# Block-sparse attention feeding a channel mixer: attention units of two query blocks of two batches, sampled values loaded by SyncE, a mixer that alternates batches

## The chip, the core and the metric

The kernel runs on one core of one Trainium2 chip. TensorE (PE) does the matrix products and the transposes, VectorE (DVE), ScalarE (ACT) and GpSimd (POOL) do the elementwise work, SyncE (SP) issues most transfers; sixteen DMA engines move the data between device memory and the on-chip memory. The metric is the time of one execution on the device in microseconds (us). A kernel's time is the median of its runs. A profiled execution also gives a span, from the first to the last instruction; the time of a run includes a little around it.

## The reference

There are 4 batches, 8 heads, 768 tokens and 64 channels a head; the tokens form 24 blocks of 32. A query block sees its own block and both neighbours, the first and the last block, and three sampled blocks; queries of the first and the last block see all keys.

```python
mask = np.abs(blk_i - blk_j) <= 1
mask = mask | (blk_i == 0) | (blk_j == 0) | (blk_i == 23) | (blk_j == 23)
for qb in range(24):
    for kb in sampled_blocks[qb]:            # three per query block, the same for all batches and heads
        mask[qb*32:(qb+1)*32, kb*32:(kb+1)*32] = True
scores = np.where(mask, 0.125 * q @ k.T, -1e9)
attn = softmax(scores)                       # row maximum taken off, sum + 1e-9 below
x = (attn @ v)                               # heads side by side: (4, 768, 512)
x_prev = x shifted by one token, zero before the first
xk = mu_k * x + (1 - mu_k) * x_prev
xr = mu_r * x + (1 - mu_r) * x_prev
kk = np.maximum(xk @ w_k, 0.0)               # 512 -> 1024
out = sigmoid(xr @ w_r) * ((kk * kk) @ w_v)  # 1024 -> 512
```

The weights come as 64-bit floats, the rest as 32-bit.

## The kernel before

**Attention units.** The work on attention is cut into units of 128 query rows. A *wide* unit (u = 0, one per batch) takes the four blocks 21, 22, 23 and 0. Blocks 21 and 22 go with the two that see all keys, and a mask does the rest; for each pair of heads (`wide_pair`) it computes scores against all 768 keys. A *near* unit (u = 1 to 5) takes four consecutive query blocks of one batch; each block of 32 rows has its own eight key blocks: three neighbours, the first and the last block, three sampled ones. `near_group` does half of the heads at a time: 32 small score matmuls per group (line 525), mask and row minimum on VectorE (line 480), exponential on ScalarE (line 490), eight transposes (line 501), their copy out (line 507), 64 value matmuls (line 547). `finish` divides by the sums (line 610), transposes (line 607) and copies into the mixer's input `xt` (line 624).

**Keys and values of a near unit.** `load_unit` brings them. For each query block SyncE issues one transfer of the three neighbour blocks' keys (line 460), one of the first and last block's keys where the slot held another batch (line 454), and three of sampled blocks (line 456), whose address SyncE works out from a register. They go into one of `KR_BUFS` = 5 slots, used in turn; a unit uses four. The neighbours' values and block 0's are one transfer by SyncE (line 469) into the first half of one of `VR_BUFS` = 6 slots; the last block's and the three sampled blocks' values are gathered by GpSimd's queue with a list of row numbers in `lines` (line 471, an indirect transfer over 128 partitions). The list is made once at the start by `find` in `mask_setup`.

**Mixer.** `mixer(b)` runs over three tiles of 256 tokens of one batch, batch after batch. A tile has two gates (`gate`, line 714), four pairs of hidden blocks (`hidden`, line 732, with ReLU at 745, square at 746, and the low part of the square at 747 and 749) and two value products (`values`, line 761), each in three terms of split precision. `split_x` makes the mixed inputs: differences (line 677, on VectorE for the tiles in `DIF_DVE`, else on GpSimd), mixes (line 681), and a high and a low part (lines 688, 690). The next tile's inputs are made during the present one. The 64-bit weights are brought by ScalarE's queue (line 352) and turned into 32-bit high and low parts by `weight` (lines 361 to 388).

**Order.** Every operation is put in a `Plan` with an engine, an expected duration, a rank and its dependences; `Plan.order` places them one after another: on each engine, among operations that can start within `NEAR` ns of the first possible one, that of lowest rank; an operation whose mode (`table`) is that of the one before is preferred by `STAY`. The order in which they are placed is the order of the instructions; on the chip each engine then works in order and waits for what it needs. `UNITS` is the order of the attention units, `unit_time` their ranks. Transfers are modelled with one rate, one delay and a completion. While TensorE has nothing to do before `SPIN_END`, idle matmuls (line 335) are put in its gaps.

`UNITS` begins with the wide units of batches 0, 1 and 2, then units 1 and 2 of batch 0, then the wide unit of batch 3, then the rest in order of batch. The results of the wide units of batches 2 and 3 are kept in device memory (`away`) until `xt` has room.

## Time and profile before

| | |
|---|---|
| median of 3 runs | 627.03 us (623.53 to 627.45) |
| profiled execution | 621.7 us span; its own time is not given apart, and the median of the runs lies 5.3 us above this span |
| PE busy | 592.3 us, 95% of the span |
| VectorE, ScalarE, GpSimd busy | 301.6, 301.5, 343.7 us |
| moved by DMA | 114.18 MB, 184 GB/s over the span |
| key transfers of sampled blocks (line 456) | 240 of 64 KB |
| value gathers by GpSimd (line 471) | 80, 79.1 us busy |

In a busy-time row by stage the columns are the stretch and its length in us, then PE, weight loads, VectorE, ScalarE, GpSimd (with the number of instructions), the granted clock, the mean share of the DMA engines and GB/s. In a timeline row they are start, duration, engine, line, operation, output and inputs, count, and in brackets the idle time before it and what ended it. In a group's row the busy time and the mean duration of one in ns stand after the first bar, the engine's idle time before these instructions after the second. A busy PE is not a PE at its peak: the ends of matmuls are modelled, and time in its pipeline counts.

### The profile page before, as it was taken

The numbers are of one execution on the slowest core, as the hardware profiler recorded it, in microseconds if no ns is written. First come the engines' busy times: TensorE is split into PE (matmuls) and PEld (weight loads), VectorE is DVE, ScalarE is ACT, GpSimd is POOL, SyncE is SP. The second block draws the span as 40 slices with busy tenths as digits, with TensorE's granted clock in tenths as the row PEclk, the third lists the DMA queues.
The fourth block names the chain that finished last, engine by engine and source line by source line (L and its number), as shares of the span: only waits on it lengthen the run. The fifth ranks groups of instructions, "written<-read, shape, count | busy, mean of one in ns | idle before, by whom it ended". The sixth has DMA issues, their size and how long they took to land.

```text
span 621.7 us, 20808 instructions
## 1 busy us (share of the span) xinstructions
PE 592.3 (95%) x8243; PEld 471.8 (76%) x8253; DVE 301.6 (49%) x906; ACT 301.5 (48%) x712; POOL 343.7 (55%) x400
## 2 busy tenths in 40 slices
PE   8799989899999999999999998999999999999997
PEld 3566655568767877877878777778778778889897
DVE  5659755787574355264353443562633531415300
ACT  3566762576643545455445535544535444243341
POOL 1215541658886647557837835546457554565551
PEclk9989999999999999999999999999999999999999
DMA  8979658948788387665765765775755620000000
GB/s 303 351 227 338 200 157 297 289 151 273 261 236 283 86 277 223 193 198 183 237 205 155 220 190 177 247 212 163 233 185 162 212 79 2 34 1 35 18 18 34
DMA packets 88499, 114.18 MB, mean 184 GB/s; under 512 B 12626, under 2 KB 59219, under 8 KB 88403
## 3 DMA queue, kind: packets, MB, share of 16 engines
q1 hardware_dynamic: 78690, 81.30, 41.1%
q0 software_dynamic: 6400, 20.98, 10.6%
q10 hardware_dynamic: 3312, 10.59, 4.9%
q8 instruction: 65, 1.06, 0.7%
q14 instruction: 32, 0.25, 0.1%
HBM read 106.01 MB, written 6.82 MB: 181 GB/s over the span
## 4 chain that ended last, share of the span: by engine, by line
PE 62%; ACT 9%; issue 7%; POOL 6%; DMA 6%; DVE 5%; SPq 2%; another core or an unknown queue 2%; ACTq 0%; POOLq 0%
PE v L761 14%; PE h_3p L732 6%; PE h_1p L732 5%; PE h_2p L732 5%; PE o L547 5%; PE r_0p L714 5%; ACT p L490 4%; PE t L501 4%; PE s L525 4%; PE r_1p L714 3%; PE h_0p L732 3%; DMA k_ring<-kq 2%; PE tw L501 2%; PE o L586 2%; POOL VR L471 2%
## 5 line engine op out<-in xcount | busy, mean ns | idle before, releaser
L761 PE MATMUL v<-wv,k 128*128 128x512 f32 (+1 forms) x600 | 140.9, 387 | 0.9 <-POOL wv L388 0.8
L761 PEld LDWEIGHTS v<-wv,k 128*128 128x128 f32 x600 | 107.1, 188 | 26.0 <-DVE xr_2f L681 1.2
L490 ACT ACTIVATE p<-p,nm 128x256 f32<-128x256 f32 x160 | 79.4, 498 | 41.8 <-DVE nm L480 35.4
L471 POOL DMA_INDIRECT VR<-vt,lines x80 | 79.1, 988 | 34.9 <-issue 15.1
L507 DVE COPY pt<-t 128x512 f32<-128x512 f32 x80 | 53.1, 685 | 68.7 <-PE t L501 65.2
L480 DVE CUSTOM_DVE_ANT_1 p<-s,near_mask 128x256 f32<-128x256 f32 x160 | 57.7, 419 | 39.2 <-remote 19.6
L690 POOL TENSOR_TENSOR xr<-xr_1f,xr 128x256 fp32r<-128x256 f32 x24 | 17.8, 740 | 69.1 <-ACT xr L688 68.9
L525 PE MATMUL s<-KR,q 64*32 64x256 f32 x1280 | 49.5, 381 | 1.3 <-issue 0.7
L501 PE MATMUL t<-ident,p 128*128 128x128 f32 x320 | 47.6, 278 | 1.0 <-ACT p L490 0.4
L547 PEld LDWEIGHTS o<-VR,pt 128*32 128x32 f32 x2560 | 37.8, 110 | 13.3 <-issue 9.5
L688 ACT CAST xr<-xr_1f 128x256 fp32r<-128x256 f32 x24 | 9.7, 406 | 73.6 <-PE r_0p L714 49.0
L547 PE MATMUL o<-VR,pt 128*32 128x64 f32 x2560 | 44.6, 221 | 0.4 <-DMA VR<-vt,lines 0.4
L732 PE MATMUL h_1p<-xk,wk 128*128 128x256 f32 x288 | 37.0, 283 | 8.0 <-ACT h_0k L745 4.7
L610 DVE TENSOR_TENSOR x<-o,R 128x512 f32<-128x512 f32 x24 | 16.6, 691 | 56.9 <-PE o L547 51.3
L501 PEld LDWEIGHTS t<-ident,p 128*128 128x128 f32 x320 | 36.0, 141 | 8.8 <-ACT p L490 5.5
L732 PEld LDWEIGHTS h_1p<-xk,wk 128*128 128x128 f32 x288 | 34.7, 188 | 10.4 <-ACT h_0k L745 5.6
L490 ACT ACTIVATE pw<-pw,nmw 128x768 f32<-128x768 f32 x32 | 29.8, 935 | 21.0 <-DVE nmw L480 16.2
L732 PEld LDWEIGHTS h_0p<-xk,wk 128*128 128x128 f32 x288 | 34.9, 188 | 3.4 <-issue 2.9
L732 PEld LDWEIGHTS h_2p<-xk,wk 128*128 128x128 f32 x288 | 34.9, 188 | 3.4 <-ACT k L746 2.9
L732 PE MATMUL h_3p<-xk,wk 128*128 128x256 f32 x288 | 37.1, 283 | 0.2 <-ACT h_2k L745 0.2
L525 PEld LDWEIGHTS s<-KR,q 64*32 64x32 f32 x1280 | 25.9, 105 | 14.8 <-issue 6.2
L732 PE MATMUL h_2p<-xk,wk 128*128 128x256 f32 x288 | 37.0, 283 | 0.0
(115 smaller groups left out, 1078.6 us busy)
## 6 DMA issues: line engine op xcount, KB each, us to landing
VR<-vw SPq DMA_DIRECT2D x80, 256.0 KB
KR<-kd SPq DMA_DIRECT2D x80, 192.0 KB
KR<-kt SPq DMA_DIRECT2D x240, 64.0 KB
k_ring<-kq SPq DMA_DIRECT2D x16, 384.0 KB
VR<-vt SPq DMA_DIRECT2D x24, 256.0 KB
q<-qt SPq DMA_DIRECT2D x23, 256.0 KB
out<-z SPq DMA_DIRECT2D x23, 256.0 KB
early_w<-w_k ACTq DMA_DIRECT2D x8, 512.0 KB
```

Source lines behind the costliest of these rows:

```text
L471: plan.add(POOL, GATHER, at - LEAD_V + 0.01 * j, lambda w=w, n=n: nc.gpsimd.indirect_dma_start(VR[w].ap[:, 1, :], None, vt.rearrange("b n ...
L480: nc.vector.tensor_tensor_reduce(out=p.ap[:, cs].rearrange("p (a x) -> p a x", x=BLK), in0=view().rearrange("p (a x) -> p a x", x=BLK), in ...
L490: plan.add(ACT, 280 + 0.83 * (cs.stop - cs.start), rank, lambda: nc.scalar.activation(p.ap[:, cs], p.ap[:, cs], AF.Exp, bias=nm.ap[:, col ...
L501: nc.tensor.transpose(tp.ap[:, i, :], p.ap[:, cs], ident.ap)
L507: plan.add(DVE, 600, rank + 0.1, lambda: nc.vector.tensor_copy(out=pt.ap, in_=tp.ap), reads=[(tp,)], writes=[(pt,)])
L525: nc.tensor.matmul(s.ap[ROWS[j], row, a * 256 : (a + 1) * 256].rearrange("p (n x) -> p n x", x=BLK), q.ap[half, hp, ROWS[j]], KR[keys[j]]. ...
L547: nc.tensor.matmul(o.ap[ROWS[j], h * D : (h + 1) * D], pts[i // 2].ap[:, 2 * (i % 2) + g, ROWS[j]], VR[values[j]].ap[:, g, h * D : (h + 1) ...
L610: plan.add(DVE, 600, rank, lambda: nc.vector.tensor_tensor(out=x.ap.rearrange("p (h d) -> p h d", d=D), in0=o.ap.rearrange("p (h d) -> p h ...
L690: plan.add(POOL, 80 + 2.4 * MIX * tw, rank + O_MIX, lambda f=f, cs=cs: nc.gpsimd.tensor_tensor(out=dst.ap[:, 1, cs], in0=f.ap, in1=dst.ap[ ...
L714: nc.tensor.matmul(pr.ap[:, 0:512], xr.ap[:, a, c, :], wr.ap[:, w, c, :], start=(c == 0 and m == 0), stop=(c == CC - 1 and m == 2))
L732: nc.tensor.matmul(ph.ap[:, ff * TT : (ff + 1) * TT], wk.ap[:, w, c, f * P : (f + 1) * P], xk.ap[:, a, c, :], start=(c == 0 and m == 0), s ...
L761: nc.tensor.matmul(pv.ap[:, 0:width], k2.ap[:, a, f, i * P : (i + 1) * P], wv.ap[:, w, f, cs], start=(f == 0 and m == 0), stop=(f == FC - ...
```

## The change

A near unit becomes two query blocks of two batches (a pair), so there are 10 units for each of the 2 pairs, still of 128 rows and with the same matmuls. A key slot holds eight blocks of both batches: twice as large, `KR_BUFS` = 2 instead of 5. A sampled key block of both batches is one transfer of 128 KB where there were two of 64 KB. A value slot holds one set of four blocks for both batches, and a unit uses two for the neighbours (one transfer of 512 KB each) and two for the last and the sampled blocks. Those are now issued by SyncE, three transfers of 128 KB a slot, each to 32 of the 128 partitions, with the same register as the keys; the last block's is brought again only where the slot held something else. GpSimd issues no gather, and `lines`, `find` and their input are gone.

The input of the mixer is kept by pair and tile of 256 tokens (three buffers of both batches) instead of by batch. The copy into it is cut in two where a unit lies across two tiles. The mixer goes through the tiles in the order (0, t0), (1, t0), (0, t1), (1, t1), (0, t2), (1, t2), (2, t0), (3, t0) and so on. The wide units stay what they were; the order of units begins with the wide ones of batches 2, 0 and 1, then the first four near units of the first pair, then the wide one of batch 3. The planner models eight transfers in flight at a time, prices leaving a mode of TensorE by the mode that is left, and all its ranks are new. All differences of the mixer's inputs are on GpSimd (`DIF_DVE` is empty). The masks of all near units are made by whole-tile instructions.

```diff
-QB, NC, SLOTS = 4, 5, 8
+QB, SLOTS = 4, 8
+PAIR = 2
+NP, NM = B // PAIR, (NB - QB) // PAIR
...
-    SWITCH = {"ACT": 1300, "PE": 110}
+    SWITCH = {"ACT": 1300}
+    LEAVE = {"scores": 300, "values": 170, "wide": 110, "whole": 90}
...
-    RING, RING_POOL, RATE, DONE = 650, 1000, 310, 670
+    RING, RATE, DONE, LANES = 650, 300, 670, 8
...
+            if op.size:
+                end = at
+                for i in range(op.parts):
+                    end = max(end, lanes[lane]) + ns / op.parts
+                    queue_free = max(queue_free, end + self.RING) + op.size / op.parts / self.RATE
+                    lanes[lane] = queue_free + self.DONE
+                    lane = (lane + 1) % self.LANES
...
-UNITS = [(0, 0), (1, 0), (2, 0), (0, 1), (0, 2), (3, 0)]
-UNITS += [(b, u) for b in range(B) for u in range(1, NC + 1) if (b, u) not in UNITS]
+UNITS = [
+    (2, ALL), (0, ALL), (1, ALL), (0, 0), (0, 1), (0, 2), (0, 3), (3, ALL), (0, 4), (0, 5), (0, 6), (0, 7),
+    (0, 8), (0, 9), (1, 0), (1, 1), (1, 2), (1, 3), (1, 4), (1, 5), (1, 6), (1, 7), (1, 8), (1, 9),
+]
+TILES = [(PAIR * p + i, t) for p in range(NP) for t in range(NT) for i in range(PAIR)]
...
-    KR = [fixed([P, SLOTS, HP * BLK], F32, f"KR{i}") for i in range(KR_BUFS)]
-    VR = [fixed([P, 2, DM], F32, f"VR{i}") for i in range(VR_BUFS)]
+    KR = [fixed([P, SLOTS, PAIR, HP * BLK], F32, f"KR{i}") for i in range(KR_BUFS)]
+    VR = [fixed([P, PAIR, DM], F32, f"VR{i}") for i in range(VR_BUFS)]
...
                 for i in range(NRAND):
-                    nc.sync.dma_start(KR[r].ap[:, 5 + i, :], kt[bass.ds(sampled_block(n, i) + b * NB, 1)].rearrange("o p x -> p (o x)"))
+                    nc.sync.dma_start(KR[r].ap[:, 5 + i].rearrange("p b x -> p (b x)"),
+                                      kt[bass.ds(sampled_block(n, i) + pr * NB, 1)].rearrange("o p x -> p (o x)"))
...
-            plan.add(SP, ISSUE, at - LEAD_V + 0.01 * j, lambda w=w, n=n: nc.sync.dma_start(VR[w].ap[:, 0, :], vw[b, n - 1]),
-                     writes=[(VR[w], 0)], release=at - LEAD_V, size=262144)
-            plan.add(POOL, GATHER, at - LEAD_V + 0.01 * j, lambda w=w, n=n: nc.gpsimd.indirect_dma_start(
-                VR[w].ap[:, 1, :], None, vt.rearrange("b n k x -> (b n k) x"),
-                bass.IndirectOffsetOnAxis(ap=lines.ap[:, b, n - 1 : n], axis=0)),
-                reads=[(lines,)], writes=[(VR[w], 1)], release=at - LEAD_V, size=262144)
+            def gather(w=far, n=n, more=more):
+                if more:
+                    nc.sync.dma_start(VR[w].ap[0:BLK].rearrange("p b x -> p (b x)"), vt[(pr + 1) * NB - 1].rearrange("k b x -> k (b x)"))
+                for i in range(NRAND):
+                    nc.sync.dma_start(VR[w].ap[(i + 1) * BLK : (i + 2) * BLK].rearrange("p b x -> p (b x)"),
+                                      vt[bass.ds(sampled_block(n, i) + pr * NB, 1)].rearrange("o k b x -> (o k) (b x)"))
+            plan.add(SP, ISSUE, at - LEAD_V + 0.01 * j, lambda w=near, n=n: nc.sync.dma_start(VR[w].ap.rearrange("p b x -> p (b x)"), vw[pr, n - 1]),
+                     writes=[(VR[near], 0, 1)], release=at - LEAD_V, size=524288)
...
-                            q.ap[half, hp, ROWS[j]], KR[keys[j]].ap[half, :, hp * BLK : (hp + 1) * BLK],
+                            q.ap[half, hp, ROWS[j]], KR[keys[j % PAIR]].ap[half, :, j // PAIR, hp * BLK : (hp + 1) * BLK],
...
-                            VR[values[j]].ap[:, g, h * D : (h + 1) * D], start=(g == 0), stop=(g == 1), skip_group_check=True)
+                            VR[values[j % PAIR][g]].ap[:, j // PAIR, h * D : (h + 1) * D], start=(g == 0), stop=(g == 1), skip_group_check=True)
...
-KR_BUFS, VR_BUFS, P_BUFS, PT_BUFS, T_BUFS, M_BUFS = 5, 6, 4, 4, 2, 1
+KR_BUFS, VR_BUFS, P_BUFS, PT_BUFS, T_BUFS, M_BUFS = 2, 6, 4, 4, 2, 1
...
-DIF_DVE = frozenset([(2, 0), (2, 1), (3, 1), (3, 2)])
-O_MAX, O_EXP, O_TR, O_PV, O_END = -5.335, 4.852, 0.824, 2.509, 0.703
-FIRST_K, LEAD_W, LEAD_Q, LEAD_K, LEAD_V = 35.035, 14.471, 9.567, 12.128, 8.904
-O_MIX, O_SQ = -5.339, -10.806
-NEAR = 94.131
+DIF_DVE = frozenset()
+O_MAX, O_EXP, O_TR, O_PV, O_END = -18.352, 15.421, 7.927, 14.932, 5.117
+FIRST_K, LEAD_W, LEAD_Q, LEAD_K, LEAD_V = 32.834, 15.273, 22.533, 12.051, 10.413
+O_MIX, O_SQ = 24.788, -13.071
+NEAR = 308.526
...
-A_FIRST, A_WIDE, A_SOON, A_STEP = 4.254, 17.894, 6.977, 20.726
-SOON, SECOND = 3, 0.36
-STAY, STORE = 3.933, 955.319
-M_FIRST, M_STEP, M_LAST = 84.0, 41.944, 446.907
+A_FIRST, A_WIDE, A_SOON, A_STEP = -6.908, 16.07, 11.323, 23.999
+SOON, SECOND = 8, 0.264
+STAY, STORE = 7.732, 0.0
+M_FIRST, M_STEP, M_LAST = 83.39, 40.819, 510.717
```

More of the change, by code (lines that the diff above doesn't have):

```diff
@@ L148, in order @@
                 for op in ops:
-                    at = max(now, op.release)
-                    for d in op.deps:
-                        at = max(at, d.end + (self.HOP[d.engine] if d.engine != engine else self.SAME.get(engine, 60)) + d.lag)
+                    at = max(now, op.ready)
                     for buf in op.bufs:
@@ L217, in block_sparse_attention_channel_mix @@
     ctx: ExitStack, tc: tile.TileContext,
[L218 removed]
+    kt, kd, kq, qw, qn, vt, vw, blocks, rows, consts, mu_k, mu_r, w_k, w_v, w_r, out, wide,
 ):
@@ L447, in load_unit, with load_near @@
+        return q, keys, values
+    def load_near(pr, m, at):
+        q = buf([P, HP, P], F32, "q", 2, f"q{pr}_{m}")
+        plan.add(SP, ISSUE, at - LEAD_Q, lambda: nc.sync.dma_start(q.ap, qn[pr, m]),
+                 writes=[(q, *range(HP))], release=at - LEAD_Q, size=262144)
+        keys, values = [], []
+        ahead = FIRST_K if (pr, m) == (0, 0) else LEAD_K
+        for j in range(PAIR):
+            n = PAIR * m + 1 + j
             r = place(0)
             keys.append(r)
-            more = slots[r] != b
@@ new lines, in finish @@
+        pr, i = divmod(b, PAIR)
+        spans = [(0, 1, 3 * BLK, P), (NT - 1, 1 + TT - 3 * BLK, 0, 3 * BLK)]
+        if not pr:
+            for t, at, lo, hi in spans:
+                plan.add(ACT, 200 + 0.83 * CC * (hi - lo), rank, lambda t=t, at=at, lo=lo, hi=hi: nc.scalar.copy(
+                    xt[pr, t].ap[:, i, :, at : at + hi - lo], tp.ap[:, :, lo:hi]), reads=[(tp,)], writes=[(xt[pr, t], (ALL, b))])
+            return
+        to = buf([P, CC, P], F32, "pt", PT_BUFS, f"hold{b}")
@@ new lines, in finish, with back @@
+        keep = away[b - PAIR]
+        plan.add(ACT, 590, rank, lambda: nc.scalar.copy(to.ap, tp.ap), reads=[(tp,)], writes=[(to,)])
+        plan.add(SP, ISSUE, rank, lambda: nc.sync.dma_start(keep.ap, to.ap), reads=[(to,)], writes=[(keep,)], size=262144)
+        for t, at, lo, hi in spans:
+            def back(rank, t=t, at=at, lo=lo, hi=hi):
+                plan.add(SP, ISSUE, rank, lambda: nc.sync.dma_start(xt[pr, t].ap[:, i, :, at : at + hi - lo], keep.ap[:, :, lo:hi]),
+                         reads=[(keep,)], writes=[(xt[pr, t], (ALL, b))], size=262144)
+            held.setdefault((pr, t), []).append(back)
@@ new lines, in block_sparse_attention_channel_mix, with touch @@
+    held = {}
+    seen = set()
+    def touch(pr, t, rank):
+        if (pr, t) in seen:
+            return
+        seen.add((pr, t))
+        if t == 0:
+            plan.add(POOL, 50, rank, lambda: nc.gpsimd.memset(xt[pr, t].ap[:, :, :, 0:1], 0.0), writes=[(xt[pr, t], "z")])
+        for back in held.get((pr, t), ()):
+            back(rank)
+    def attention():
+        for i, (b, m) in enumerate(UNITS):
+            t0, t2 = unit_time(i), unit_time(i + 1)
+            name = f"{b}_{m}"
+            o = buf([P, DM], F32, "o", 1, f"o{name}", ps)
+            L = buf([P, H], F32, "L", 4, f"L{name}")
+            if m == ALL:
+                q, keys, values = load_wide(b, t0 if i else A_FIRST - 24)
@@ L811, in mixer @@
             plan.add(ACT, 1040, at(13), sigmoid, reads=[(z[0],), (z[1],)], writes=[(z[0],), (z[1],)], table="sigmoid")
-            for i in range(2):
-                values(b, t0, i, k2, z[i], last, at(15.6 + 5.2 * i), rate)
+            for half in range(2):
+                values(b, t0, half, k2, z[half], last, at(15.6 + 5.2 * half), rate)
     mask_setup()
@@ L817, in block_sparse_attention_channel_mix @@
     weights()
-    for b in range(B):
-        mixer(b)
+    mixer()
     before = None
```

317 lines of the change are left out of this document (144 added, 173 removed).

## The prediction

> **What bounds the kernel now.** I read the page first, for its span and its forty slices, then the busy time by stage, then the chain of waits for what one piece costs when nothing is in its way, and last the timelines of TensorE and SyncE around the place where the mixer starts.
>
> ```profile
> span 621.7 us, 20808 instructions
> ...
> PE 592.3 (95%) x8243; PEld 471.8 (76%) x8253; DVE 301.6 (49%) x906; ACT 301.5 (48%) x712; POOL 343.7 (55%) x400
> ...
> PE   8799989899999999999999998999999999999997
> ...
> DMA  8979658948788387665765765775755620000000
> ```
>
> The span is 621.7 us. The median of the runs shown is 627.03, so 5.3 us lie around the span; I make the sum on the span and add 5.3. TensorE looks busy in nearly every slice, but its record also covers waiting inside the pipeline, so I ask what it delivered. In the DMA slices the transfers are dense for the first third and absent in the last sixth.
>
> ```profile
> 0.00:121.40 121.40, 107.58 (x1966) 68.78 (x1977) 78.79 (x242) 68.66 (x152) 42.41 (x59) 0.97 0.80 270
> 121.40:139.70 18.30, 16.94 (x495) 12.24 (x493) 15.15 (x42) 12.26 (x25) 11.80 (x15) 1.00 0.52 170
> 139.70:180.00 40.30, 38.35 (x575) 30.98 (x568) 27.54 (x68) 22.28 (x57) 33.23 (x37) 1.00 0.82 258
> 180.00:520.00 340.00, 330.99 (x4567) 272.38 (x4566) 153.67 (x490) 165.50 (x422) 204.96 (x240) 1.00 0.62 193
> 520.00:621.70 101.70, 98.40 (x653) 87.41 (x651) 26.41 (x68) 32.77 (x59) 51.29 (x52) 1.00 0.06 22
> ```
>
> The columns are TensorE matmuls, weight loads, VectorE, ScalarE, GpSimd, then the clock, the DMA share and the rate. What each piece costs back to back comes from the chain of waits (start, duration, line, count), first its front and then its tail:
>
> ```profile
> 51.54 1.49 PE sw L564 x8
> ...
> 57.56 1.04 PE tw L501 x8
> ...
> 70.88 1.48 PE o L586 x96
> ...
> 96.56 1.03 PE o L547 x64
> ...
> 136.71 1.02 PE s L525 x32
> ...
> 142.83 0.44 PE tx L607 x4
> ...
> 147.62 0.87 PE t L501 x8
> ```
>
> ```profile
> 551.58 10.90 PE v L761 x48
> 562.48 2.82 PE h_0p L732 x24
> 565.30 2.80 PE r_0p L714 x12
> ```
>
> A mixer tile is 48 value matmuls (10.90), four pairs of hidden blocks (4 x 2.82) and two gates (2 x 2.80): 27.8 us. A near unit is 64 score matmuls (2 x 1.02), 16 transposes (2 x 0.87), 128 value matmuls (2 x 1.03) and its last four transposes (0.44): 6.3 us. A wide unit is 4 x 1.49 + 6 x 1.04 + 4 x 1.48 + 0.44 = 18.6 us. Twelve tiles, 20 near units and four wide ones: 333 + 126 + 74 = 533 us. So about 88 us of the span are not TensorE work, and no part of the diff changes the 533. The question is only where the 88 lie.
>
> ```profile
> 79.34 1.10 PE L525 MATMUL s<-KR,q 64*32 64x256 f32 x32 [0.48 <-PE tw L501]
> ...
> 82.35 1.66 PE L525 MATMUL s<-KR,q 64*32 64x256 f32 x32
> ...
> 86.42 1.55 PE L586 MATMUL o<-VR,ptw 128*32 128x64 f32 x96
> ...
> 101.16 1.49 PE L525 MATMUL s<-KR,q 64*32 64x256 f32 x37
> ...
> 113.65 0.60 PE L607 MATMUL tx<-ident,x 128*128 128x128 f32 x4 [0.16 <-DVE x L610]
> ...
> 121.45 3.05 PE L714 MATMUL r_0p<-wr,xr 128*128 128x512 f32 x12
> ...
> 139.73 3.10 PE L732 MATMUL h_0p<-xk,wk 128*128 128x256 f32 x24
> ```
>
> From 139.73 on, mixer work is always at hand. Before that the wide units and two near units had been done:
>
> ```profile
> 0.00:139.70 139.70, 27.94 (x1536) 23.90 (x1536) 0.98 0.76 257
> ```
>
> ```profile
> 0.00:139.70 139.70, 7.83 (x192) 3.69 (x192) 0.98 0.76 257
> ```
>
> The first row is line 586 (all 1,536 wide value matmuls are done), the second line 525 (three near units' scores). With the matching transposes and one gate (2.8) TensorE had delivered 74 + 2 x 6.3 + 2.0 + 2.8 = 91 us by 139.7: 48 us are lost in front. The tail from 520 on is TensorE work end to end (the three rows of the tail above are from there, and 551.58 + 10.90 is where the next one starts), so it loses nothing, and the other 40 us lie between 139.7 and 520.
>
> **The front, part by part.** The first mixer tile needs two near units now; in the change two batches come ready together, so it needs four, and the fourth wide unit comes after them. What paces near units in a row? Scores of one unit begin at 79.34, of the next at 101.16: 21.8 us. SyncE in between:
>
> ```profile
> 83.45 0.33 SPq L460 DMA_DIRECT2D KR<-kd  x1
> ...
> 92.64 1.69 SPq L456 DMA_DIRECT2D KR<-kt  x3
> ...
> 96.39 0.34 SPq L426 DMA_DIRECT2D q<-qt  x1
> ```
>
> After the last scores (82.35 + 1.66 = 84.0) SyncE sends the next keys from 83.45 to 94.33, then the queries at 96.39, and the scores start 4.8 us behind those. The change halves the key transfers of a unit (two neighbour and six sampled ones for 4 and 12, each twice as wide): half of those 10.9 us goes, 5.4, and the larger lead of the queries takes up to 2.0 more (96.39 - 94.33). The period becomes 14.4; if the new value transfers get in between it stays at up to 21.8. There is no spare key slot any more (two instead of five), but in the old ring, too, three of four blocks waited for the scores. Fourth near unit's scores: 79.3 + 3 x 14.4 = 122.5; last transposes 12.5 later (113.65 - 101.16), first gate 7.8 after that (121.45 - 113.65): 143. By then TensorE has done three wide units (55.7), four near units (25.1) and as much of the fourth wide unit as VectorE lets through.
>
> ```profile
> L480 DVE CUSTOM_DVE_ANT_1 p<-s,near_mask 128x256 f32<-128x256 f32 x160 | 57.7, 419 | 39.2 <-remote 19.6 <-PE s L525 16.7 <-PE r_1p L714 2.9
> L507 DVE COPY pt<-t 128x512 f32<-128x512 f32 x80 | 53.1, 685 | 68.7 <-PE t L501 65.2 <-PE o L547 2.2 <-DMA away<-hold 0.7
> ...
> L480 DVE CUSTOM_DVE_ANT_1 pw<-sw,wide_mask,nmw 128x384 f32<-128x384 f32 x32 | 18.5, 612 | 4.4 <-PE sw L564 4.2
> ...
> L480 DVE CUSTOM_DVE_ANT_1 pw<-sw,wide_mask 128x384 f32<-128x384 f32 x32 | 16.8, 552 | 4.8 <-PE tw L501 4.0 <-PE sw L564 0.6
> ```
>
> VectorE was busy 78.8 + 15.2 = 94 us up to 139.7. Two more near units add at least 2 x (57.7 + 53.1) / 20 = 11, the fourth wide unit without its masks takes away (18.5 + 16.8) / 4 = 8.8. With the whole of that wide unit VectorE would be 105 of 143 us busy, 73% against 67% now. I take two thirds of the wide unit as done, 12 us: 143 - 55.7 - 25.1 - 12 = 50 lost, against 48. I count the front at 0; its ends are -5 (the whole wide unit fits) and +14 (the rival below).
>
> **The middle.**
>
> ```profile
> L471 POOL DMA_INDIRECT VR<-vt,lines x80 | 79.1, 988 | 34.9 <-issue 15.1 <-PE o L547 14.7 <-PE o L586 2.4
> ...
> L732 PE MATMUL h_1p<-xk,wk 128*128 128x256 f32 x288 | 37.0, 283 | 8.0 <-ACT h_0k L745 4.7 <-issue 2.4 <-ACT p L490 0.9
> ...
> L677 POOL TENSOR_TENSOR xk_2d<-xt 128x256 f32<-128x256 f32 x12 | 7.2, 615 | 0.4 <-DVE xk_2f L681 0.4
> ```
>
> Sampled values no longer go through GpSimd: 80 gathers of 988 ns leave its queue, 79 us in all. What was behind them there is the preparation of the next tile (lines 677 and 690) and the squares (747, 749). Their waits:
>
> ```profile
> POOL VR L471 <- PE o L547: 14.7, 8, 8.6
> ```
>
> 14.7 us in eight waits, at most 8.6, in which GpSimd stood still with mixer work queued behind. GpSimd is 60% busy between 180 and 520 (204.96 of 340), so most of its loss is covered by TensorE's other work; if that cover is gone it is worth the whole 14.7. I take 4. Against it, the differences of four tiles go from VectorE to GpSimd: 48 operations of at most 0.62, under 30 us, beside 79 freed; nothing.
>
> The new ranks put ReLU and square ahead of the exponentials (the offset of the first falls from -10.8 to -13.1, of the second rises from 4.9 to 15.4). The second hidden block's row shows 8.0 us of idle TensorE, mostly waiting for ScalarE's first hidden block, which stands behind four exponentials. I take 6 of the 8; below, nothing; above, 8. What is late next is the transposes of that near unit, with value matmuls there to fill.
>
> The planner now prices leaving each TensorE mode and prefers longer to stay. The remaining 32 us of the middle are such changes and short waits; a tenth of it, 3, is my estimate, from a loss of 6 (exponentials too late, tiles short of work) to a gain of 8.
>
> On SyncE a unit sends 6 dynamic value transfers for 6 dynamic key transfers saved (3 take 1.69), so its time stays as it was. The added wait is that of these value transfers on the preceding value matmuls; behind it stand the next keys, the queries and the output stores, and the score matmuls wait for those. The neighbour values waited on the same matmuls at the same place before, so nothing; the other end is the 8.6 above. The extra pieces of the copy to the mixer's input (four more copies of part of a tile) lie on a ScalarE that is half idle (165.50 of 340). Alternating batches in the mixer changes no instruction; the tail still holds at least the two tiles that need the last unit, and stays full.
>
> Values now land in 32 partitions at a time.
>
> ```profile
> q0 software_dynamic: 6400, 20.98, 10.6%
> ```
>
> 20.98 MB took 10.6% of 621.7 us, 65.9 us on all engines, 3.1 us per MB. The new sampled values are 15.7 MB (120 times 128 KiB): 49 us. If a 32-partition transfer holds the engines twice as long, 49 more are spread over the span; in the middle the share is 0.62 and hides its part, in front (0.80) four units' 3.1 MB add up to 10. The Trainium skill has such a rule ("SBUF — State Buffer", Door 1: The DMA port swizzle): 32 partitions reach 8 of 16 ports, with about half the rate. No transfer of this trace is so narrow; by that rule the sum would be 624 instead of 614.
>
> **Sum.** 621.7 + 0 - 4 - 6 - 3 = 608.7, with 5.3 around it 614.
>
> **The rivals.** *More than that:* the planner's DMA lanes also keep the early key loads out of the way of the wide units, the near period falls to 11, and the gate starts at 133: with the same two thirds 40 lost, -8 in front, and 5 more of the middle: 601. For it: VectorE has room. Chance 0.17.
> *Nothing:* one set of short waits for another, 627. For it: TensorE is the bound and its 533 stay. Chance 0.20.
> *Slower: the mixer starves at its start.* The near period stays at 21.8, because SyncE now carries the values between keys. Scores of the fourth unit at 144.7, first gate at 165; TensorE has done 55.7 + 25.1 + 18.6 and some 3 of a fifth unit, 102: 63 lost, +15, and of the middle's 13 only 4 come: 638. It decides from a period of about 18.7, where 3 x 4.3 eat the 13. Against it: the key transfers are halved. Chance 0.18.
> *The narrow values* hold the engines in front, as above: 624. Chance 0.06. The forecast has 0.39.
>
> **How the numbers follow.** A measurement here can tell about 1% from no change: 620.8 and 633.3 are the bounds. The forecast's own range, 603 to 625, is faster in 0.33 of its 0.39; with the first rival and a little of the others faster gets 0.52, the same 0.27 (most of *nothing*, the narrow values, the rest of the forecast), slower 0.21. The range takes in the first rival's 601 with some room and most of the slow one: 598 to 638.
>
> **What would show it.** Near scores in the front at a period near 14 us and the first gate near 143; a GpSimd queue without gathers and with under 300 us of work; no idle time at the second hidden block; a tail of full slices after the last near unit. The prediction is wrong if the first hidden blocks come after 160, if SyncE's waits for value matmuls hold key loads, or if TensorE's lost time between there and the last unit isn't under 30 us.

## The result, and the profile after

The kernel before took 627.42 us beside it (median of 12 runs, 623.53 to 629.97), the changed kernel 623.87 (12 runs, 614.38 to 630.08). The ratio of 0.986 [0.982, 0.990], about 1.4% faster, leaves out the seven of the changed kernel's twelve runs that lie over 1.5% above its fastest; the two medians, over all runs, give 0.994. Run again later as `after2`, beside 13 runs of the kernel before (626.01), it took 622.06 (617.18 to 628.44), ratio 0.992 [0.988, 0.996], and the medians again give 0.994. So the change gains 0.6 to 1.4%, and whether it is more than 1% is not settled.

> The changed kernel once more, for a second profile beside the experiments. Both theories: a ratio near 0.986 to the kernel before; the first hidden blocks between 145 and 163 us, where the kernel before has them at 139.7; a near period of some 15 to 20 us in the front (70.6, 85.7, 105.8, 126.1 in the profile at hand).

The profile taken with the result has a granted clock of 0.983 (own time 623.73, span 622.0); the lines below are from `after2`, with 0.994 (own time 618.72, span 616.9). Its page, as for the kernel before:

```profile
span 616.9 us, 20533 instructions
...
PE 585.6 (95%) x8267; PEld 476.2 (77%) x8281; DVE 291.0 (47%) x850; ACT 300.7 (49%) x716; POOL 287.0 (47%) x360
...
PE   9999899698889999799999999999999999999997
...
DMA  8896788898879576875557447575384420000000
```

The span is 4.8 us shorter than before's 621.7, VectorE and GpSimd have less to do (291.0 and 287.0 us for 301.6 and 343.7), and the last sixth of the DMA slices is empty as before. By stage, with the cuts at the first gate, the first hidden block, 200 and 520 us (columns: TensorE matmuls, weight loads, VectorE, ScalarE, GpSimd, clock, DMA share, GB/s):

```profile
0.00:122.20 122.20, 107.53 (x2154) 71.94 (x2169) 73.84 (x235) 65.47 (x154) 26.93 (x37) 0.98 0.83 266
122.20:157.20 35.00, 31.15 (x707) 22.43 (x705) 21.96 (x71) 22.21 (x55) 9.45 (x13) 0.96 0.89 272
157.20:200.00 42.80, 37.32 (x497) 30.00 (x490) 37.48 (x90) 26.98 (x73) 29.26 (x32) 1.00 0.88 263
200.00:520.00 320.00, 316.09 (x4354) 268.12 (x4353) 138.64 (x414) 156.44 (x383) 164.42 (x208) 1.00 0.56 166
520.00:616.90 96.90, 93.48 (x569) 83.69 (x567) 19.05 (x41) 29.62 (x55) 56.90 (x71) 1.00 0.06 22
```

The timeline of TensorE shows where the mixer starts (start, duration, line, operation, count, idle time before it):

```profile
70.11 1.96 PE L538 MATMUL s<-KR,q 64*32 64x256 f32 x64
...
85.67 1.96 PE L538 MATMUL s<-KR,q 64*32 64x256 f32 x64
...
105.74 1.51 PE L538 MATMUL s<-KR,q 64*32 64x256 f32 x45
109.84 1.05 PE L538 MATMUL s<-KR,q 64*32 64x256 f32 x19 [2.59 <-issue]
...
122.29 2.83 PE L744 MATMUL r_0p<-wr,xr 128*128 128x512 f32 x6
125.04 1.96 PE L538 MATMUL s<-KR,q 64*32 64x256 f32 x64
126.93 1.67 PE L744 MATMUL r_0p<-wr,xr 128*128 128x512 f32 x6
...
157.28 3.14 PE L762 MATMUL h_0p<-xk,wk 128*128 128x256 f32 x24
```

The first gate comes at 122.29, in two halves, and the first hidden block at 157.28, against 121.45 and 139.73 before. What had been done by then, from the same busy-time view for three lines alone, the wide value matmuls (line 599), the near scores (538) and the near value matmuls (560):

```profile
0.00:157.20 157.20, 25.16 (x1488) 22.01 (x1488) 0.98 0.84 267
```

```profile
0.00:157.20 157.20, 11.02 (x320) 6.13 (x320) 0.98 0.84 267
```

```profile
0.00:157.20 157.20, 8.47 (x512) 7.50 (x512) 0.98 0.84 267
```

That is 1,488 of 1,536 wide value matmuls, the scores of five near units, the values of four and one gate: 74.4 - 0.7 + 4 x 6.3 + 2.0 + 2.8 = 103.7 us by the prices of the prediction. So 157.2 - 103.7 = 53.5 us are lost in front, where the kernel before lost 48. The 533 us of TensorE work being the same, 616.9 - 533 = 83.9 are lost in all, and 30.4 of them after the first hidden block, where it lost 40. By this pair of profiles the change costs 5 us in front and saves 10 behind. The profile taken with the result has the same work done and its first hidden block at 162.59, 5.3 us later than `after2`, and 459.4 us from there to its end, against 459.6: what the front costs differs between executions by as much as its own size.

### The profile page after: what moved, and what is told of

The parts are those of the page before. It is cut to its first block, busy times and chain, and to the rows that moved or that the text cites. A ratio compares the mean times of both kernels' runs of the same rounds, so it can differ in the third digit from the quotient of the medians.

```text
span 622.0 us, 20533 instructions
## 1 busy us (share of the span) xinstructions
PE 589.5 (95%) x8267; PEld 479.7 (77%) x8281; DVE 291.8 (47%) x850; ACT 301.0 (48%) x716; POOL 287.1 (46%) x360
## 3 DMA queue, kind: packets, MB, share of 16 engines
q1 hardware_dynamic: 51730, 96.63, 51.7%
q8 instruction: 65, 1.06, 0.7%
## 4 chain that ended last, share of the span: by engine, by line
PE 83%; DVE 6%; issue 5%; DMA 3%; SPq 2%; ACT 1%; ACTq 0%; DVEq 0%
PE v L791 20%; PE s L538 6%; PE r_0p L744 6%; PE o L560 5%; PE h_2p L762 5%; PE h_3p L762 5%; PE h_1p L762 5%; PE h_0p L762 5%; PE r_1p L744 5%; PE t L515 4%; PE tw L515 4%; PE sw L577 3%; PE idle L334 3%; DMA KR<-kt 2%; PE tx L618 2%
## 5 line engine op out<-in xcount | busy, mean ns | idle before, releaser
L791 PE MATMUL v<-wv,k 128*128 128x512 f32 (+1 forms) x600 | 137.9, 385 | 0.7 <-POOL wv L387 0.4
L538 PE MATMUL s<-KR,q 64*32 64x256 f32 x1280 | 46.8, 399 | 8.9 <-issue 6.5
L560 PE MATMUL o<-VR,pt 128*32 128x64 f32 x2560 | 42.3, 220 | 3.5 <-issue 3.3
L515 PE MATMUL t<-ident,p 128*128 128x128 f32 x320 | 44.4, 280 | 0.3 <-PE tx L618 0.2
L515 PEld LDWEIGHTS t<-ident,p 128*128 128x128 f32 x320 | 38.3, 145 | 5.3 <-ACT p L504 1.1
L799 DVE SCALAR_TENSOR_TENSOR z<-v,z 128x512 f32<-128x512 f32 (+1 forms) x25 | 16.7, 668 | 50.8 <-PE v L791 29.5
L762 PEld LDWEIGHTS h_3p<-xk,wk 128*128 128x128 f32 x288 | 36.3, 194 | 3.3 <-ACT h_2k L775 2.3
L744 PE MATMUL r_0p<-wr,xr 128*128 128x512 f32 x144 | 37.9, 412 | 0.0
L519 ACT COPY ptw<-tw 128x512 f32<-128x512 f32 x48 | 26.6, 588 | 23.1 <-PE tw L515 17.7
L762 PE MATMUL h_0p<-xk,wk 128*128 128x256 f32 x288 | 37.4, 285 | 0.2 <-ACT z L751 0.2
```

The costliest lines, as they stand in the source:

```text
L515: nc.tensor.transpose(tp.ap[:, i, :], p.ap[:, cs], ident.ap)
L519: plan.add(ACT, 490, rank + 0.1, lambda: nc.scalar.copy(pt.ap, tp.ap), reads=[(tp,)], writes=[(pt,)])
L538: nc.tensor.matmul(s.ap[ROWS[j], row, a * 256 : (a + 1) * 256].rearrange("p (n x) -> p n x", x=BLK), q.ap[half, hp, ROWS[j]], KR[keys[j % ...
L560: nc.tensor.matmul(o.ap[ROWS[j], h * D : (h + 1) * D], pts[i // 2].ap[:, 2 * (i % 2) + g, ROWS[j]], VR[values[j % PAIR][g]].ap[:, j // PAI ...
L744: nc.tensor.matmul(pr.ap[:, 0:512], xr.ap[:, a, c, :], wr.ap[:, w, c, :], start=(c == 0 and m == 0), stop=(c == CC - 1 and m == 2))
L762: nc.tensor.matmul(ph.ap[:, ff * TT : (ff + 1) * TT], wk.ap[:, w, c, f * P : (f + 1) * P], xk.ap[:, a, c, :], start=(c == 0 and m == 0), s ...
```

## Experiments

They were timed in four sets, each on one chip together with the kernel before; ratios compare within a set. In the first three the kernel before took 626.01, 624.32 and 626.74 us, in the last 610.71. Unless something else is said the order of every engine is that of the changed kernel.

**Sampled values of full width (`wide_values`).** Is a transfer to 32 partitions slow? Here each goes to all 128, 1 KB in each, so that the sampled keys meet other values.

```diff
-nc.sync.dma_start(VR[w].ap[(i + 1) * BLK : (i + 2) * BLK].rearrange("p b x -> p (b x)"),
-                  vt[...].rearrange("o k b x -> (o k) (b x)"))
+nc.sync.dma_start(VR[w].ap[:, i % 2, i // 2 * (DM // 2) : (i // 2 + 1) * (DM // 2)],
+                  vt[...].rearrange("o k b (c x) -> (o k b c) x", c=2))
```

> The sampled values are brought in the same number of transfers of the same 128 KB by the same queue in the same order, but spread over 128 partitions (rows of 1 KB) instead of 32 (rows of 4 KB), so that they stand in the wrong places and the attention's result is left wrong; nothing else changes. Theory N (the narrow transfers hold the DMA engines and the keys behind them land late): the median time to landing of these transfers falls from 5.3 us to about 4, the stall of 3.4 us inside the third near unit's scores goes, the first hidden blocks come 5 to 10 us earlier, and the time falls by 4 to 8 us, to a ratio of 0.973 to 0.980. Theory K (two key slots without a spare one pace the near units, whatever the width): the first hidden blocks stay within 3 us, the ratio within 0.004 of the changed kernel's.

615.28 us (613.43 to 618.83), ratio 0.982 [0.974, 0.990]; `after2` ran in the same set with 622.06. The median is 6.8 us lower, as the first theory had it, though the two intervals overlap; the spans of the profiles are 5.2 apart. From the two pages, `after2` first: the large queue (packets, MB, share of 16 engines) and the landing of the value transfers (count, KB each, us):

```profile
q1 hardware_dynamic: 51730, 96.63, 51.9%
...
VR<-vt SPq DMA_DIRECT2D x129, 128.0 KB, 4.9
```

```profile
q1 hardware_dynamic: 64114, 96.63, 49.5%
...
VR<-vt SPq DMA_DIRECT2D x129, 128.0 KB, 4.2
```

The same 96.63 MB held the engines 51.9% of 616.9, 320 us, and 49.5% of 611.7, 303 us; a transfer lands 0.7 us sooner. So the narrow transfers cost 17 us of engine time more than these wide ones. But the rows changed too, from 4 KB to 1 KB. The next kernel, `pool_same`, brings the sampled values in rows of 4 KB over 128 partitions, by another queue; its page:

```profile
q1 hardware_dynamic: 45538, 79.72, 38.5%
q0 software_dynamic: 5760, 20.97, 10.0%
```

Of its 619.0 us, 38.5% are 238 us for the 79.72 MB of everything else. If these cost the same in `after2`, its other 16.91 MB, the narrow values, held the engines the remaining 82 us, 4.8 us per MB, where the gathers take 62 us for 20.97 MB, 3.0 per MB; the wide rows of 1 KB come to 3.8 by the same working. By this estimate a narrow transfer holds the engines 1.6 times as long as a wide gather, some 32 us more in all, where the prediction had 49 for twice as long (the same working with `ring7_pool_ns` below gives 4.9 and 2.9 us per MB). The Trainium skill ("SBUF — State Buffer", Door 1: The DMA port swizzle) gives a transfer to partitions 0 to 31 half of the ports; the trace agrees on the direction, at 1.6 and not 2. But the first hidden block came at 155.85, only 1.4 earlier, where the theory had 5 to 10; of the 5.2 us between the spans 3.8 lie behind that block.

**Gathers by GpSimd again (`pool_same`).** All sampled values come by 40 gathers of 512 KB on GpSimd, as wide as before the change.

```diff
+lines = ...                          # row numbers, made once
-for i in range(NRAND): nc.sync.dma_start(VR[w].ap[(i + 1) * BLK : ...], vt[...])
+nc.gpsimd.indirect_dma_start(VR[w].ap..., None, vt..., IndirectOffsetOnAxis(ap=lines.ap[:, pr, n - 1 : n], axis=0))
```

> The changed kernel with its order of instructions on every other engine, but each block's sampled values of both batches come in one indirect gather on GpSimd's queue (40 of 512 KB, over 128 partitions) instead of three transfers by SyncE (120 narrow ones). My step that the gathers off GpSimd are worth 4 us: 40 gathers are half of the old 80, so 1 to 3 us are lost in the middle. Theory N: the front gains 4 to 8 us, as with full-width values, so 2 to 6 us faster than the changed kernel, ratio 0.976 to 0.983. Theory K with my step: 1 to 3 us slower, ratio 0.988 to 0.991.

619.58 us (617.49 to 621.02), ratio 0.986 [0.979, 0.993]. The group of gathers, and TensorE's first hidden block:

```profile
L494 POOL DMA_INDIRECT VR<-vt,lines x40 | 40.0, 1000 | 41.1 <-PE o L579 28.8
```

```profile
158.81 3.14 PE L781 MATMUL h_0p<-xk,wk 128*128 128x256 f32 x24
```

From 158.81 to the end of its 619.0 us are 460.2 us, with the gathers; 616.9 - 157.28 = 459.6 without. GpSimd waits 28.8 us on value matmuls in these gathers, with mixer work behind them, and TensorE loses nothing measurable by it. The ratio lies between those of the two theories, and the first hidden block is not earlier than in `after2`: neither was borne out.

**The fourth wide unit earlier (`w3_early`)**, between the second and the third near unit, planned anew:

```diff
-(0, 0), (0, 1), (0, 2), (0, 3), (3, ALL), (0, 4)
+(0, 0), (0, 1), (3, ALL), (0, 2), (0, 3), (0, 4)
```

> The fourth wide unit stands between the second and the third near unit instead of behind the fourth, with the order planned for it. If TensorE's loss in front is waiting for the keys and values of near units (both theories), the wide unit's 18.6 us of work fill it: 4 to 8 us less lost before the mixer, ratio 0.973 to 0.980. Rival (VectorE paces the front, as my two thirds of the wide unit had it): the mixer starts later by as much as is filled, and the ratio stays within 0.004 of the changed kernel's or goes above it.

637.41 us (632.05 to 639.74), ratio 1.013 [1.004, 1.022], the first hidden block at 177.68 us. The work done up to there is that of `after2` but for the 48 last wide value matmuls, so some 20 us more are lost; the granted clock is 0.93 up to there, against 0.98. Moving the wide unit forward did not fill the front. That is the sign that the rival had named, but the order was planned anew, so it does not show that VectorE paces the front.

**Fewer bytes (`light_both`, `light_free`), and no dummies (`no_spin`).** In the second to fifth near unit one sampled key block and one sampled value block are loaded instead of three; and the dummy matmuls that the planner puts into gaps of TensorE are left out after the planned 80 us.

```diff
-for i in range(NRAND):                                    # keys, and the same for values
+for i in range(1 if pr == 0 and 1 <= m <= 4 else NRAND):  # light_both, light_free
...
-if before is not None and warm.start < op.start <= cold.start:
+if before is not None and warm.start < op.start <= min(cold.start, 80e3):   # light_free, no_spin
```

> The changed kernel with two of the three sampled key loads and two of the three sampled value loads left out in the second to fifth near unit of the first pair (32 transfers of 128 KB, 4.2 MB; what an earlier unit left stands in their place, so the sampled part of those units is not computed). The order on every engine is the same, and the dummy matmuls stay. Theory (the bytes pace the front: 0.72 to 0.99 of the DMA engines' time is taken from 40 to 160 us, at 228 to 295 GB/s): 4.2 MB at 240 GB/s are 17 us, of which the dummy matmuls, whose number is fixed, keep some 7; first hidden block at 143 to 150 instead of 157.3, time 609 to 616 us. Rival (TensorE's own order, or another engine, paces the front): first hidden block at 154 to 158, time within 3 us of the changed kernel's 622 to 624.

> The same loads left out, and the 49 dummy matmuls that the changed kernel issues after the planned 80 us left out too (10.4 us of TensorE at 213 ns). Theory (bytes pace the front): first hidden block 2 to 6 us earlier than with the dummies, at 138 to 147, if the clock holds; time 606 to 614. Rival: first hidden block at 154 to 158.

> The changed kernel without those 49 dummy matmuls, all loads in. If loads are what TensorE waits for there, the dummies only fill the wait: first hidden block within 2 us of 157.3, or later by what half clock costs, time 621 to 628. Rival (the dummies, planned at one and a half times the gap, themselves delay the front): first hidden block 4 to 9 us earlier, time 612 to 618.

`light_both` took 614.48 us (ratio 0.982 [0.977, 0.988]), `light_free` 606.54 (0.969 [0.962, 0.976]), `no_spin` 618.85 (0.991 [0.987, 0.994]). Their first hidden blocks, in that order:

```profile
158.35 3.14 PE L762 MATMUL h_0p<-xk,wk 128*128 128x256 f32 x24
```

```profile
149.64 3.14 PE L762 MATMUL h_0p<-xk,wk 128*128 128x256 f32 x24
```

```profile
159.91 3.14 PE L762 MATMUL h_0p<-xk,wk 128*128 128x256 f32 x24
```

Taking 4.2 MB away does nothing for the start of the mixer (158.35), nor does taking the dummies away (159.91); both together bring it to 149.64, 10.3 earlier than without the dummies alone. That lies between the forecasts of the theory (138 to 147) and of the rival (154 to 158), though the time is as the theory had it. The dummies are a fixed number, made for the gaps of the plan. Between 70 us and the first hidden block the profiles of `after2` and `light_both` list no wait of TensorE for a DMA transfer, that of `no_spin` 4.5 us, that of `light_free` 0.5. So with the dummies in its queue TensorE does not wait for loads, and without them it does. Of the 10.3 us, then, 4.0 are waits for loads. In the rest, three stretches of half clock fewer (two for five, 3.4 us each) can make up to 5.1, and the stops of the last section 0.8. Fewer loads do bring the mixer forward once the dummies are gone; that bytes alone pace the front isn't shown, since the 32 transfers left out shorten SyncE's queue as well. `light_both` missed its forecast (143 to 150). Of its 8 us below `after2` in time some 3 lie behind the first hidden block by the two profiles; the two were not timed in one set, and the rest stays open.

**The ranks (`old_ranks`, `sq_late`).** The forecast put 6 us on ReLU and square standing ahead of the exponentials.

```diff
-O_EXP ... = 15.421; O_SQ = -13.071
+O_EXP ... = 4.852; O_SQ = -10.806      # old_ranks: both as before the change
+O_SQ = 10.0                            # sq_late: ReLU of a tile's first block 5 behind exp, as before
```

> The changed kernel with the ranks of exp and of ReLU and square as they were before the change (4.852 and -10.806), planned with them. Theory (these ranks took the idle time off the second hidden block): the idle time before that block goes from 1.3 back to 6 to 9 us, time 626 to 632. Rival (the alternating batches or the lighter GpSimd took it): it stays under 3 us, time within 3 us of the changed kernel's.

> The changed kernel with the rank offset of ReLU and square at +10 instead of -13.1 (exponentials stay at 15.4), so that the first hidden block's ReLU stands 5 behind the exponentials as it stood before the change; planned with it, and the order differs in some 70 places. Theory (the ranks took the idle time at the second hidden block): it goes from 1.4 back to 5 to 8 us, time 3 to 6 us over the changed kernel's. Rival (the alternating batches and the lighter queues took it): under 3 us, time within 2 us of it.

`old_ranks` took 653.54 us (1.046 [1.037, 1.054]), `sq_late` 628.96 (1.004 [1.001, 1.008], beside `ring7` below with 0.994 in the same set). `old_ranks` is another order from its front on (first near scores at 84.06 us), so its time says little of the ranks alone. The row of the second hidden block (busy, mean ns, idle time before it) in both, `old_ranks` first:

```profile
L762 PE MATMUL h_1p<-xk,wk 128*128 128x256 f32 x288 | 37.3, 285 | 0.0
```

```profile
L762 PE MATMUL h_1p<-xk,wk 128*128 128x256 f32 x288 | 37.4, 285 | 0.0
```

No idle time at this block in either: the theory falls at its place. `sq_late` differs from the changed kernel in some 70 places. It has the first hidden block at 156.42 and 466.0 us from there, 6.4 more than 459.6; in its waits of TensorE a new one leads the list:

```profile
PE t L515 <- DVE pt L521: 4.1, 2, 3.3
```

Against `ring7` in its set it is 6.2 us slower. So these ranks may be worth about what was forecast, but not at that block; and its profile has a granted clock of 0.83 from 160 to 200 us, which can cost up to 40 x 0.17 = 6.8 us, so how much is order and how much clock isn't told apart.

**A seventh value buffer (`ring7`), and the front put together (`ring7_pool_ns`, `pool_front_ns`).** A near unit fills four of six value buffers, so two loads of the next one wait for its value matmuls on SyncE, and the keys behind them. The second kernel adds gathers by GpSimd for the first five near units and has no dummies after the planned 80 us; the third is the same with six buffers.

```diff
-VR = [... for i in range(VR_BUFS)]          # 6, used in turn
+VR = [... for i in range(7)]                # ring7: 0, 2, 4 neighbours, 1, 3, 5, 6 sampled; a wide unit the longest unused
...
+if (pr, m) <= (0, 4): nc.gpsimd.indirect_dma_start(VR[w].ap..., lines...)   # the other two
```

> The changed kernel with seven value buffers instead of six (three for neighbour values, four for sampled ones; a wide unit takes the longest unused), with the order of every engine as it was. A near unit fills four of them, so with six two loads of the next unit wait for this unit's value matmuls, and on SyncE the keys stand behind them (value loads at 93.79, 104.77 and 120.61 us, keys behind the first at 97.03 to 100). Theory (this loop, value matmuls to loads to next value matmuls, paces the front): with seven, one neighbour load waits and no sampled one; near periods of 19 to 20 us become 16 to 18, first hidden block at 150 to 155, time 614 to 619 us. Rival (the bytes alone pace it): first hidden block at 156 or later, time 620 to 624.

> The same seven buffers, and for the first five near units the sampled values by one GpSimd gather of 512 KB each in place of three or four transfers into 32 partitions on SyncE, and no dummy matmuls after the planned 80 us. Theory: SyncE carries 30 dynamic value transfers less between the keys, the transfers are of full width, and nothing fixed fills the time that is won; first hidden block at 142 to 151, time 606 to 614. Rival (bytes alone): first hidden block at 154 or later, time 617 to 622, with more half clock than with the dummies.

> The last kernel with six value buffers instead of seven: for the first five near units one GpSimd gather of 512 KB per sampled value tile, no dummy matmuls after the planned 80 us. Theory (the narrow transfers and SyncE's queue hold the front, the seventh buffer does little, as alone): first hidden block at 148 to 154, time 610 to 615 us, ratio to the kernel before 0.974 to 0.984. Rival (the buffer is needed once the rest is out of the way): first hidden block at 156 to 160, time 616 to 621, as without the dummies alone (618.85).

`ring7` took 622.76 us (0.994 [0.990, 0.997]) with the first hidden block at 161.65: the buffer alone does nothing, as the rival had it. `ring7_pool_ns` in the same set took 612.32 (608.02 to 612.88), ratio 0.978 [0.973, 0.982]: 2.2% under the kernel before, 1.7% under `ring7`, and within its theory's forecast. Its timeline:

```profile
73.50 1.96 PE L570 MATMUL s<-KR,q 64*32 64x256 f32 x64
...
89.75 1.96 PE L570 MATMUL s<-KR,q 64*32 64x256 f32 x64
...
104.94 2.03 PE L570 MATMUL s<-KR,q 64*32 64x256 f32 x64
...
116.50 2.10 PE L570 MATMUL s<-KR,q 64*32 64x256 f32 x64
...
150.93 3.13 PE L794 MATMUL h_0p<-xk,wk 128*128 128x256 f32 x24
```

The near scores follow each other by 16.3, 15.2 and 11.6 us, and the first hidden block comes at 150.93 with the same work done (1,488 wide values, five scores, four values, one gate). Busy time from 80 to 140 us of the kernel before, `after2` and `ring7_pool_ns`:

```profile
80.00:140.00 60.00, 53.95 (x1202) 35.87 (x1191) 39.60 (x121) 33.66 (x85) 27.80 (x35) 1.00 0.70 228
```

```profile
80.00:140.00 60.00, 51.44 (x1036) 36.01 (x1042) 33.25 (x107) 24.61 (x80) 8.49 (x13) 0.94 0.89 255
```

```profile
80.00:140.00 60.00, 48.15 (x1127) 35.81 (x1131) 37.62 (x123) 30.21 (x91) 20.56 (x27) 0.97 0.91 317
```

With nearly the same share of the engines, 0.91 for 0.89, 317 GB/s are moved instead of 255.

`pool_front_ns` took 612.46 us (609.48 to 616.67) in the last set, where the kernel before took 610.71 (608.1 to 616.0): ratio 1.002 [0.999, 1.005]. The first hidden block came at 152.45, as forecast, and the time is in the forecast range; the forecast ratio isn't, since on that chip the kernel before is 2.5% faster than on the other three. Why is not known: no profile of it is from there. By the two profiles, of two chips, the seventh buffer brings 1.5 us in front. That `ring7_pool_ns` is faster than the kernel before is shown for one chip only, and the gain of the change itself only where the kernel before takes 626 to 627 us.

## Why the prediction was right, and where its steps were not

The time, 623.87, lies 9.9 us above the forecast 614 and inside 598 to 638. Faster by over 1% had the most chance, 0.52. The measurements give 1.4% and 0.8%, and 0.6% by the medians, so the range held, while faster by over 1% is not settled. Step by step:

**TensorE's work and the tail.** The matmuls are the same, as said; the time in which TensorE is busy with them isn't (see the middle). From 520 us on `after2` has 96.9 us, with 93.48 of TensorE busy, and still does attention up to 518: the tail stays full.

**5.3 us around the span.** The profile with the result has 623.73 for a span of 622.0, so 1.7 us lie around it. The rest of the 5.3 was the difference between one execution and the median. By 1.7 the sum would have been 610.4 for an execution like the profiled one.

**The front at 0, ends -5 to +14.** Measured +5 (53.5 for 48), and more in the profile with the result, which has the first hidden block at 162.59. The step that failed is the near period of 14.4: the scores follow at 15.6, 20.1 and 19.3, 18.3 on average, next to the 18.7 from which the starving mixer was to decide; the front lies between the forecast and that rival. Three periods cost 11.7 us more than the sum had. Against that the first near scores start at 70.11 and not at the 79.3 that the sum took from the kernel before, 9.2 earlier, which is in no term: the fourth unit's scores come at 125.04, near the forecast 122.5, by luck. The argument for the short period was that half of the key transfers go. It left unpriced that the first tile of two batches needs the bytes of two. The view of the DMA queues up to the first hidden block, before and `after2`:

```profile
DMA packets 21795, 35.99 MB, mean 257 GB/s; under 512 B 3062, under 2 KB 11342, under 8 KB 21767
```

```profile
DMA packets 19616, 41.97 MB, mean 267 GB/s; under 512 B 2854, under 2 KB 7591, under 8 KB 19585
```

5.98 MB more were moved, 22 us at the second's 267 GB/s, and the block comes 17.5 us later. This fits, but it proves nothing by itself: a later block leaves more time for loads of every sort. The added wait on SyncE was counted at nothing (the queue's waits over the whole run, before and `after2`: us in total, times, longest):

```profile
SPq L469 <- PE o L547: 15.8, 12, 3.8
```

```profile
SPq L485 <- PE o L560: 71.9, 15, 11.9
```

It grew from 15.8 to 71.9 us, but 67.9 of that lie between 157.2 and 520 us, where TensorE's waits for DMA come to 3.3; from 70 us to the first hidden block it is 4.0 us, and 2.0 before the change. So it did not make the front late, and a buffer more didn't help by itself. The narrow values, +10 in front and 624 in all as a rival of 0.06: two thirds of the estimate on the engines (32 us for 49) and 6.8 in time by `wide_values`, which at 615.28 comes near the forecast 614; but little of it is at the first hidden block, where the rival had put it.

Another difference of the front is in no term. TensorE's waits that the profile calls "issue" add up to 0.7 us from 70 us to the first hidden block before and to 10.1 in `after2` (6.3 in `no_spin`, 5.5 in `light_free`, 3.1 in `ring7_pool_ns`), and in the same stretch `after2` has two stretches of half clock, the kernel before none. The stops alone are larger than the 5 us; the two half-clock stretches of 3.4 us can cost up to 3.4. So what set the place of that block is not settled: `light_free` (149.64, fewer bytes) and `ring7_pool_ns` (150.93, all bytes, moved faster) speak for bytes and their rate, but both also have fewer of these stops, and a shorter queue on SyncE.

The first gate at 143 was wrong in another way: a gate covers half a tile and needs two near units, not four, so it came at 122.29; only the hidden blocks need all four. The loss forecast there, 50 up to 143, is 53.5 up to 157.2, with the whole fourth wide unit done.

**The middle at -13.** Measured -10 (30.4 for 40), but hardly any of it is less waiting. By the busy times of the stages TensorE was busy 369.3 of the middle's 380.3 us before, so idle 11.0, and is busy 353.4 of 362.8 in `after2`, so idle 9.4. The work there, by the prediction's prices, is 340.3 us before (380.3 - 40) and 332.4 now (362.8 - 30.4). So 29 us of busy time beyond the work became 21: 8 of the 10 us. The whole run shows it too, once the dummies are taken out of the busy time; their rows, before and `after2`:

```profile
L335 PE MATMUL idle<-const-bfloat16-1.0 128*128 128x512 bf16 x91 | 25.0, 403 | 1.7 <-PEq L870 0.8 <-issue 0.5 <-DMA q<-qt 0.2
```

```profile
L334 PE MATMUL idle<-const-bfloat16-1.0 128*128 128x512 bf16 x115 | 31.4, 407 | 1.7 <-PEq L899 0.8 <-issue 0.6
```

Without them TensorE is busy 592.3 - 25.0 = 567.3 us before and 585.6 - 31.4 = 554.2 after: 13.1 less for the same matmuls. These stand in fewer and longer runs. Counted in the two traces, 346 unbroken runs of matmuls of one source line became 295; a run of 64 scores takes 1.96 us (above), one of 32 takes 1.10 (the prediction's row at 79.34). So the term that was mis-sized is the mode changes, at -3: fewer and longer runs are worth some 8 in the middle. Whether the new prices, the other ranks or the alternating batches made the runs longer was not told apart.

The gathers, -4: nothing; `pool_same` has them back (40 wide ones for 80) and loses nothing. The second hidden block, -6: its idle time is gone, 8.0 us before (2.4 of them "issue", which no rank explains) and now

```profile
L762 PE MATMUL h_1p<-xk,wk 128*128 128x256 f32 x288 | 37.4, 285 | 1.4 <-ACT h_0k L775 1.4
```

but not by these two ranks, as the two experiments say, and other waits took its place, since the idle time of the middle fell by only 1.6 in all. The lighter GpSimd is unlikely: `pool_same`, with half of the gathers back, shows the same row with 1.4. What is left is the alternation of batches, the mode prices and the other ranks; none was run alone, so it stays open.

**The signs.** Period near 14: wrong after the first. Gate near 143: wrong. GpSimd under 300 us: right, 287.0. No idle time at the second hidden block: right to 1.4. A full tail: right. Hidden blocks after 160 would have made it wrong: 157.28 here, 162.59 in the profile with the result, on the edge. SyncE's waits for value matmuls, another such sign, grew to 71.9 us, but TensorE's waits for the keys behind them come to 1.9. Under 30 us lost in the middle was asked; 30.4 were.

So the sum came out near because a front that was 5 worse and a middle that was 3 less good than said are small beside the range, not because its terms were each right: in front a slower pace met an earlier start, and in the middle the smallest term made up for the two larger ones. That is luck.

## What to carry to other kernels

Before a unit of work is widened to several batches, count the bytes that must have landed before the next stage can start, and set them against the rate of that stretch; halving the number of transfers says nothing about that. Filler work of a fixed amount can hide a gain of the loads beneath it (here none showed with it, 10.3 us without it), so test loads and filler together. When time was won, compare the busy time of the same work before looking at waits: here most of the gain was in it. And test the parts of a planned kernel with the order held fixed: two ranks changed and planned anew moved this one by 5%.

## What the runs showed of the hardware

**The clock falls in the front.** TensorE's granted clock fell to half in stretches of 3.4 or 6.8 us, in the front. Busy time of `after2`, columns as above:

```profile
100.00:120.00 20.00, 13.90 (x322) 9.39 (x327) 7.58 (x27) 5.33 (x19) 3.02 (x6) 0.91 0.83 231
120.00:140.00 20.00, 18.06 (x307) 12.73 (x303) 12.25 (x42) 9.55 (x28) 1.70 (x3) 0.91 0.99 295
```

Over the single microsecond from 112 us the clock reads 0.50; 0.91 of 20 us is one stretch of 3.4, two in this run (from 111.2 and 121.5 us); the profile with the result has four. The runs of the changed kernel follow it: 614.38 us at a mean clock of 0.997, 618.99 at 0.994, 630.08 at 0.984. The Trainium skill ("TensorE: Matmul & The Clock Gate", Why this matters for your kernels) warns of gaps over some 3 us; the trace agrees in kind, but here the two falls came behind stops of 2.59 and 2.85 us. Yet the dummies that should prevent it bought no time: `no_spin`, at a clock of 0.981 to 0.997, was no slower relative to the kernel before (0.991) than the changed kernel (0.992).

**TensorE stops inside an operation.** In the timeline above, the scores of one near unit break off after 45 of 64 matmuls and go on 2.59 us later, with nothing that the profile shows as awaited. The changed kernel's waits of this sort, and what is left in `ring7_pool_ns` of the second:

```profile
PE o L560 <- issue: 5.2, 3, 2.8
PE s L538 <- issue: 4.3, 2, 2.6
```

```profile
PE o L592 <- issue: 0.4, 1, 0.4
```

`pool_same`, with gathers but the dummies kept, still shows 2.5 and 1.4. The queue that brings the instructions (its page row has 65 packets, 1.06 MB) shares the DMA engines. In `after2` one of its packets runs from 107.15 to 108.42 us and one from 117.60 to 118.52; the stops last from 107.25 to 109.84 and from 117.01 to 119.86, so they end 1.42 and 1.34 us after a packet has landed. The same holds throughout: the 13 profiles of the changed kernel and its variants show, from 20 us on, 63 stops of this sort of 1 us or more, and every one ends 1.2 to 1.7 us after such a packet has landed, though these are some 9 us apart on average. So TensorE very likely stood waiting for its instructions; why they came late, and whether the loads beside them delayed them, isn't shown.

**One kernel, two speeds.** The same kernel before takes 624 to 627 us on the chips of the first three sets and 610.71 on that of the last, with granted clocks of 0.991 to 1.0 there and 0.988 to 1.0 on the others.
